# Attention and expert layer on one core: the next batch's key work moves into columns that score tiles leave empty, expert counts are read from PSUM at once, and turned logits come one slot later

## The chip, the cores and the metric

The kernel runs on 1 core of one Trainium2 chip, as one program. The metric is the device time in microseconds (us), the median of several executions. Five engines work side by side and meet at semaphores: TensorE (PE; its weight loads are shown as PEld), VectorE (DVE), ScalarE (ACT), GpSimd (POOL) and SyncE (SP), which here only starts transfers. Each engine runs its own instructions strictly in the order of the program.

## The reference

```python
B, C, Hh, Ww = (4, 128, 384, 32)                     # 4 batches of 12288 tokens, 128 wide
kv_pool = kv.reshape(B, H//4, 4, W//4, 4, C).mean(axis=(2, 4))
k = v = kv_pool.reshape(B, -1, C) @ w_sr             # 768 keys a batch, keys and values alike
s = scale * (q @ k.transpose(0, 2, 1));  s = s - s.max(-1, keepdims=True)
a = np.exp(s);  a /= a.sum(-1, keepdims=True) + 1e-09
x = (a @ v).reshape(B * S, D)
logits = x @ w_gate;  e_idx = np.argmax(logits, axis=1)     # 8 experts, one a token
gate_w = softmax(logits)[e_idx];  eom = sigmoid(x @ w_output_gate)
out[e_idx == e] = gate_w * eom[:, e] * (np.maximum(x @ w1[e], 0) @ w2[e])   # 128 -> 1024 -> 128
```

## The kernel before

**Groups, steps, slots.** The 49152 tokens are cut into 96 groups of 512, 24 to a batch. The main loop takes one group `i` a step; a step has 8 slots `s`, and `now[0]` is `8 * i + s`. Products are made of high and low fp16 halves, so that three matmuls stand for one in fp32. In one step TensorE makes the scores of group i (`qk`, one block `j` of 128 tokens in each even slot, six matmuls of 384 columns), the products with the values of group i-1 (`pv`, 18 matmuls of 512 columns in slots 5 and 6), and the expert layer of group i-2, a column block `f` a slot: `moe_h` (H, first layer), and four to five blocks later `moe_y` (Y, second layer).

**One expert ahead of the others.** For each batch the kernel picks one expert from the mean of its keys (`choice`, `chosen`), loads its weights, splits them into halves (`w_split`: fp16 tiles w0 and w1, high halves on ScalarE, low halves on GpSimd) and runs it on every token. Tokens that chose another expert are put in lists in `scr` (`routing`) and done at the end.

**PSUM.** A score tile `S` is two banks of 512 columns, and its matmuls fill columns 0 to 383 of each. Columns 384 to 511 stay free; for blocks j of 2 and 3 they take the turned output of an earlier group (`moe_turn`), for blocks 0 and 1 they can take other small products: a list `hooks` holds functions with the slot from which they may run, and `qk` takes at most one for a tile. The pool `psA` has two buffers for these tiles, taken in turn; whoever asks for a tile waits until everything that read the tile two requests earlier is done. H, U (attention output), logits and turned logits share the three banks of `psH`.

**The order on each engine** is the order in which this Python code issues, with a queue to each engine: in a slot the letters of `ORD` ("shxryfue") go through scores, moe_h, exponentials, rounding, moe_y, values and at last `e`, the functions noted for this slot with `at`. After these come the generators: the weights' split, the next keys (`kp`, one piece a slot), and the routing.

**A score block's chain** is: six matmuls into S; DVE takes the largest (`nm`, L489 and L490); ACT the exponentials into `pr` (L504), which reads S last for blocks 0 and 1; ACT rounds (`ph`, L517), POOL makes the low half (L518), SP turns it (PT). For blocks 2 and 3 DVE also scales the turned output out of S (`o`, L825). In moe_h ACT makes HH (L795) and DVE makes HL (L796) from H.

**The next batch's keys** (`kv_prep`, `fast=False`) are made in steps 1 or 2 to about 20 of each batch but the last, six blocks `k` of 128 keys. POOL adds up 16 pixels (L296 to L300); 5 slots later TensorE turns the sums into a psA tile of its own, `kvt` (L304); ACT scales them into `pT` (L307); two slots later TensorE multiplies with `wsr` into another psA tile, `kvk` (L239), and ACT stores kT (L240). At the end the largest key is spread over partitions through a third kind of tile, `vmp` (L330), and the keys are split into fp16 halves K2 and turned into V2.

**The routing** (`routing`) runs for 4 groups (a unit) at a time, 25 units in all: `logits` at slot 1 of a step copies its product to `lgp` on ACT (L563), and `logits_turn`, RG = 1 slot later, turns it on TensorE (`lT`, L581). Then the generator's pieces follow: L (L611), the one-hot choice `oh` (L637), `counts` (two small matmuls of oh16 into an S tile by a hook, L642), later a copy of the counts `cnt` on DVE (L667), and at last `st` (L684) and `nd` (L695), which read that copy and the running list ends `ebase`.

Of the kernel before, what the change touches and what calls it, by code (L numbers as in the profile page):

```python
# [20 lines left out]
F32 = mybir.dt.float32  # L21
# [4 lines left out]
AF = mybir.ActivationFunctionType  # L26
ALU = mybir.AluOpType
# [3 lines left out]
ts = bass.ts  # L31

P = 128
C = 128
E = 8
# [19 lines left out]
class Cfg:  # L55
# [11 lines left out]
    RM = 1  # L67
    LAST = (3, 1)
    SK, SO = 30, 15
    RG = 1  # L70
    RSEQ = (1, 2, 1, 1)
    HJ = (0, 1)
    LC = (2, 1)
# [27 lines left out]
def body(ctx, tc, q, kv, w_sr, w_gate, w_og, w1, w2, out, cfg=Cfg):  # L101
    nc = tc.nc
    pe, act, dve, pool, sp = nc.tensor, nc.scalar, nc.vector, nc.gpsimd, nc.sync
    NB, NCH = cfg.NB, cfg.NC
    NG = NB * NCH * CG
# [12 lines left out]
    rt = ctx.enter_context(tc.tile_pool(name="rt", bufs=1))  # L118
    psA = ctx.enter_context(tc.tile_pool(name="psA", bufs=2, space=PSUM))
# [7 lines left out]
    ident = cst.tile([P, P], F32, name="ident")  # L127
    make_identity(nc, ident)
    wsr = cst.tile([P, C], F32, name="wsr")
# [9 lines left out]
    w8 = cst.tile([P, E], F32, name="w8")  # L139
# [3 lines left out]
    ebase = cst.tile([P, E], F32, name="ebase")  # L143
# [24 lines left out]
    def largest(m, ps):  # L168

        dve.tensor_reduce(out=m, in_=ps, op=ALU.max, axis=AX.X)  # L170
        dve.scalar_tensor_tensor(m, m, 2.0 ** -100, m, op0=ALU.max, op1=ALU.max)
# [27 lines left out]
    KVN = [[0, 0] for _ in range(NB)]  # L199
# [31 lines left out]
    def kv_prep(b, fast):  # L231

        kT = kvp.tile([P, NK], F32, tag="kT", bufs=1, name=f"kT{b}")
        mx = kvp.tile([P, 8], F32, tag="vmx", name=f"vmx{b}")
        vs = kvp.tile([P, NKB], F32, tag="vs", name=f"vs{b}")
        def keys(k, ps, pT):

            kk = ts(k, P)
            pe.matmul(ps[:, 1, 0:P], wsr, pT, start=True, stop=True)  # L239
            act.activation(kT[:, kk], ps[:, 1, 0:P], AF.Copy, accum_out=vs[:, k:k + 1])  # L240
# [33 lines left out]
        for k in range(NKB):  # L274
            while KVN[b][0] < 4 * (k + 1) or not fast and now[0] < KVI[(b, k)] + cfg.KVD:
                yield
            if fast:
                if k + 1 < NKB:
                    kv_add(b, k + 1)
                x, y = kvst.pop((b, k))  # L280
                ps = psA.tile([P, 2, 512], F32, tag="A", name=f"kvt{b}_{k}")
                for h, v in enumerate((x, y)):
                    for m in range(4):
                        pe.matmul(ps[:, 0, 0:P], v[:, 0, ts(m, P)], ident, start=(h == 0 and m == 0), stop=(h == 1 and m == 3))
                pT = kvp.tile([P, P], F32, tag="pT", name=f"pT{b}_{k}")
                act.activation(pT, ps[:, 0, 0:P], AF.Copy, scale=1.0 / 16.0)
                if last:
                    keys(*last)
                last = (k, ps, pT)
                if k < NKB - 1:  # L290
                    yield
                continue
            x, y = kvst.pop((b, k))
            for v in (x[:, 1, :], y[:, 0, :], y[:, 1, :]):
                spare["n"] += 1
                pool.tensor_tensor(x[:, 0, :], x[:, 0, :], v, op=ALU.add)  # L296
                yield
            spare["n"] += 1
            pool.tensor_tensor(x[:, 1, 0:256], x[:, 0, 0:256], x[:, 0, 256:512], op=ALU.add)
            pool.tensor_tensor(y[:, 1, 0:128], x[:, 1, 0:128], x[:, 1, 128:256], op=ALU.add)  # L300
            for _ in range(5):
                yield
            ps = psA.tile([P, 2, 512], F32, tag="A", name=f"kvt{b}_{k}")
            pe.transpose(ps[:, 0, 0:P], y[:, 1, 0:128], ident)  # L304
            KVN[b][1] += 1
            pT = kvp.tile([P, P], F32, tag="pT", name=f"pT{b}_{k}")
            act.activation(pT, ps[:, 0, 0:P], AF.Copy, scale=1.0 / 16.0)  # L307
            yield
            yield
            keys(k, psA.tile([P, 2, 512], F32, tag="A", name=f"kvk{b}_{k}"), pT)  # L310
            yield
        e2 = kvp.tile([P, 7], F32, tag="ve2", name=f"ve2{b}")

        if fast:
# [9 lines left out]
        mxb = kvp.tile([P, P], F32, tag="pT", name=f"mxb{b}")  # L324
        dve.tensor_copy(mxb, mx[:, 6:7].to_broadcast([P, P]))
        if not fast:
            for _ in range(3):
                yield
        ps = psA.tile([P, 2, 512], F32, tag="A", name=f"vmp{b}")
        pe.transpose(ps[:, 0, 0:P], mxb, ident)  # L330
        if fast:
            mean()
            choice(ps[:, 1, 0:E])
            next(QP[1])
            warm(cfg.WM[1])
        largest(e2[:, 5:6], ps[:, 0, 0:P])
        powers(e2[:, 0:1], e2[:, 1:2], e2[:, 5:6])
        dve.tensor_scalar(e2[:, 2:3], e2[:, 1:2], 2.0 ** 14, None, op0=ALU.mult)
        if fast:
# [119 lines left out]
        dve.tensor_tensor(qf[:, 1, :], ps, qf[:, 0, :], op=ALU.subtract)  # L459

    hooks, now, mid = [], [0], [False]
    spare = {"n": 0}

    def qk(i, j):
# [118 lines left out]


    WF = {}
    SCT = set()

    def bc(ap2, n):
# [5 lines left out]
    def routing(c):  # L594
        g0, ng = UN[c]
# [4 lines left out]
        cho = CHO[bt]  # L600
# [5 lines left out]
        def T3(nm, n=E, bufs=1):  # L606
            return T(nm, n, F32, bufs).rearrange("p (b e) -> p b e", e=n)
# [7 lines left out]
        vs = KVT[bt][3]  # L615
# [23 lines left out]
        ps = []  # L639

        def counts(S):
            pe.matmul(S[:, 0, 384:384 + E], ones16, oh16, start=True, stop=True)  # L642
            pe.matmul(S[:, 1, 384:384 + E], tri16, oh16, start=True, stop=True)
            ps.append(S)

        ending = g0 + ng + 2 >= NG
        cnt = rt.tile([P, 2, E], F32, tag="cnt", name=f"cnt{c}")
        if ending:
            for _ in range(cfg.LC[c == NU - 1]):
                yield  # L650
            counts(psA.tile([P, 2, 512], F32, tag="A", name=f"cps{c}"))
            dve.tensor_copy(cnt, ps[0][:, :, 384:384 + E])
        else:
            hooks.append((now[0] + 1, counts))
        se = T("se")
        dve.tensor_reduce(out=se, in_=dn, op=ALU.add, axis=AX.X)
        zz = T3("dn")
# [5 lines left out]
        act.activation(z, z, AF.Exp, scale=-1.0)  # L663
        while not ps:
            yield
        if not ending:
            dve.tensor_copy(cnt, ps[0][:, :, 384:384 + E])  # L667
        yield
        dve.scalar_tensor_tensor(z, z, 1.0, sume, op0=ALU.add, op1=ALU.mult)
        dve.scalar_tensor_tensor(z, se, EPS, z, op0=ALU.add, op1=ALU.mult)  # L670
# [9 lines left out]
        x = T("x0", E)  # L680
        dve.tensor_tensor_scan(x, runs[ng], ohf, 0.0, op0=ALU.mult, op1=ALU.add)
        yield
        st = rt.tile([P, E], F32, tag="st", name=f"st{c}")
        dve.scalar_tensor_tensor(st, cnt[:, 1, :], -1.0, ebase, op0=ALU.add, op1=ALU.add)  # L684
        x1 = T3("x1")
        dve.tensor_tensor(x1, x.rearrange("p (e b) -> p b e", e=E), bb(st, nb), op=ALU.add)
        dve.tensor_tensor(x1, x1, oh, op=ALU.mult)
# [3 lines left out]
        idx = T("idx", 1, I32, 3)  # L691
        dve.scalar_tensor_tensor(idx, sel, BIG, ix, op0=ALU.mult, op1=ALU.add)

        nd = rt.tile([P, E], F32, tag="nd", name=f"nd{c}")
        dve.scalar_tensor_tensor(nd, w8, cho, cnt[:, 0, :], op0=ALU.not_equal, op1=ALU.mult)  # L695
        dve.tensor_tensor(ebase, ebase, nd, op=ALU.add)
        rw = T3("rw", RW, 3)
        pool.tensor_copy(rw[:, :, 0:1], scl.unsqueeze(2))
        for n, t0, b in ((1, tok0, CT * cc), (2, row0, 2 * CT * cc), (3, row0, 2 * CT * cc + GB)):
# [286 lines left out]
    with tc.manual_schedule(engines={pool.engine, sp.engine, pe.engine, act.engine, dve.engine}):  # L986
# [24 lines left out]
        rts, kl, kp, ws = [], None, None, None  # L1011
# [5 lines left out]
        def k0(i):  # L1017
            return cfg.KV0[min(i // GPB, 1)]

        events = {}  # L1020

        def at(n, f, *args):
            events.setdefault(8 * i + s + n, []).append((f, *args))

        def after_values(ri, rc):
            if rc is not None:
                logits(rc)

                def turn():
                    logits_turn(rc)  # L1030
                    rts.append([routing(rc), 0, rc])
                at(cfg.RG, turn)
            n = max(0, 8 * cfg.UD + cfg.UDS * ri - now[0])
            at(cfg.UT + n, u_turn, ri)
            at(cfg.UO + n, u_out, ri)
# [34 lines left out]
        for i in range(NG + OL):  # L1070
            att = i < NG
            pvi, ri, mi, oi = i - 1, i - 2, i - LAG, i - OL - 1
# [153 lines left out]
```

## Time and profile before

| what | value |
|---|---|
| time, median of 3 runs (lowest to highest) | 1962.98 us (1962.57 to 1963.02) |
| profiled execution: its own time, span from first to last instruction | 1944.66 us, 1942.9 us |
| granted TensorE clock, mean | 0.993 |
| busy: PE, PEld | 1870.8 us (96%), 951.0 us (49%) |
| busy: DVE, ACT, POOL | 1504.7 us (77%), 1321.3 us (68%), 1159.8 us (60%) |
| DMA: bytes, mean rate | 311.63 MB, 160 GB/s |

A busy share is the share of the span in which an engine was executing. TensorE's matmuls overlap, and their ends are modelled, so a gap in its row is time in which nothing ran there at all.

### The profile page before, as it was taken

How to read it: one execution, taken by the hardware profiler on the slowest of the kernel's cores; microseconds unless marked ns; L12 is line 12 of the kernel's file. 1: busy time of each engine (PE TensorE's matmuls, PEld its weight loads, DVE VectorE, ACT ScalarE, POOL GpSimd, SP SyncE). 2: the span in 40 equal slices, each digit the busy share in tenths (PEclk: the TensorE clock that was granted, in tenths of full speed). 3: DMA queues.
4: the chain of work that ended last, by engine and by line, in shares of the span. 5: the costliest groups of instructions: out<-in, count | busy, mean ns of one | idle time of the engine just before them, and what ended most of it. 6: DMA issues, size and time to landing. Idle time of an engine off the chain costs nothing. (4 is left out here: it accounts for less than half of the span.)

```text
span 1942.9 us, 31028 instructions
## 1 busy us (share of the span) xinstructions
PE 1870.8 (96%) x10225; PEld 951.0 (49%) x10225; DVE 1504.7 (77%) x3005; ACT 1321.3 (68%) x2391; POOL 1159.8 (60%) x996
## 2 busy tenths in 40 slices
PE   6999999999999999999999999999999999999997
PEld 4444455454445544545444554444445555545544
DVE  6776877888878778788787787787877877877773
ACT  3767767676776766676767776667677767767653
POOL 2537566564675676754756656656466456466462
PEclk9999999999999999999999999999999999999999
DMA  8877788788988887878788988778778778786642
GB/s 234 161 153 160 168 163 180 153 163 169 183 170 165 170 178 159 168 145 187 141 168 172 187 174 169 162 155 151 167 148 167 152 147 166 154 159 142 133 105 70
DMA packets 884017, 311.63 MB, mean 160 GB/s; under 512 B 827584, under 2 KB 833857, under 8 KB 883856
## 3 DMA queue, kind: packets, MB, share of 16 engines
q1 hardware_dynamic: 870944, 309.18, 78.7%
q0 software_dynamic: 12480, 0.40, 0.5%
q8 instruction: 81, 1.33, 0.3%
q14 instruction: 80, 0.66, 0.1%
q10 hardware_dynamic: 432, 0.07, 0.0%
HBM read 56.83 MB, written 51.25 MB: 56 GB/s over the span
## 5 line engine op out<-in xcount | busy, mean ns | idle before, releaser
L518 POOL TENSOR_TENSOR ph<-pr,ph 128x768 f16<-128x768 f32 x384 | 633.0, 1649 | 629.5 <-ACT ph L517 383.2
L796 DVE SCALAR_TENSOR_TENSOR HL<-H,HH 128x512 f16<-128x512 f32 x768 | 526.0, 686 | 142.3 <-ACT HH L795 127.9
L795 ACT ACTIVATE HH<-H 128x512 f16<-128x512 f32 x768 | 456.5, 594 | 246.6 <-PE H L792 240.3
L504 ACT ACTIVATE pr<-S,nm,qm 128x768 f32<-128x768 f32 x384 | 381.0, 992 | 240.2 <-DVE nm L490 222.7
L705 POOL DMA_INDIRECT scr<-rw,idx x384 | 383.1, 998 | 95.8 <-issue 88.1
L489 DVE TENSOR_REDUCE nm<-S 128x1 f32<-128x768 f32 x384 | 365.3, 951 | 86.8 <-PE S L487 86.3
L540 PE MATMUL U<-PT,V 128*128 128x512 f16 (+1 forms) x1746 | 406.1, 378 | 7.4 <-DVE HL L796 5.1
L517 ACT ACTIVATE ph<-pr 128x768 f16<-128x768 f32 x380 | 319.9, 842 | 2.4 <-DMA PT<-ph 1.9
L790 PE MATMUL H<-U,w 128*128 128x512 f16 x768 | 292.3, 381 | 12.3 <-DVE HL L796 7.0
L791 PE MATMUL H<-U,w 128*128 128x512 f16 x768 | 292.1, 380 | 0.0
L807 PE MATMUL Y<-HL,w 128*128 128x512 f16 x768 | 291.3, 379 | 0.7 <-DVE HL L796 0.6
L792 PE MATMUL H<-U,w 128*128 128x512 f16 x768 | 291.7, 380 | 0.0
L805 PE MATMUL Y<-HH,w 128*128 128x512 f16 x768 | 291.4, 379 | 0.3 <-ACT ys L810 0.3
L806 PE MATMUL Y<-HH,w 128*128 128x512 f16 x768 | 291.3, 379 | 0.0
L540 PEld LDWEIGHTS <-V 128*128 128x128 f16 x1746 | 171.4, 98 | 212.6 <-issue 11.5
L483 PE MATMUL S<-K,qT 128*128 128x384 f16 x768 | 189.2, 328 | 13.1 <-ACT pr L504 7.5
L487 PE MATMUL S<-K,qT 128*128 128x384 f16 x768 | 189.0, 328 | 1.3 <-DVE qT L459 1.0
L485 PE MATMUL S<-K,qT 128*128 128x384 f16 x768 | 188.9, 328 | 0.5 <-DVE K L349 0.5
L825 DVE TENSOR_TENSOR o<-S,msw 128x256 f32<-128x256 f32 x176 | 74.8, 425 | 89.0 <-ACT pr L504 87.6
L792 PEld LDWEIGHTS <-w 128*128 128x128 f16 x768 | 75.3, 98 | 91.4 <-issue 1.4
L807 PEld LDWEIGHTS <-w 128*128 128x128 f16 x768 | 75.2, 98 | 90.8 <-issue 0.3
L805 PEld LDWEIGHTS <-w 128*128 128x128 f16 x768 | 75.2, 98 | 88.3 <-issue 0.5
(209 smaller groups left out, 1865.4 us busy)
## 6 DMA issues: line engine op xcount, KB each, us to landing
kvs<-in_kv_dram SPq DMA_DIRECT2D x96, 256.0 KB
q<-in_q_dram SPq DMA_DIRECT2D x96, 256.0 KB
urows<-uT SPq DMA_DIRECT2D x96, 256.0 KB
out_dram<-o SPq DMA_DIRECT2D x96, 256.0 KB
PT<-ph SPq DMA_TRANSPOSE x384
scr<-rw,idx POOLq DMA_INDIRECT x384
wr<-in_moe_w_dram SPq DMA_DIRECT2D x8, 512.0 KB
tw<-in_moe_w_dram SPq DMA_DIRECT2D x4, 512.0 KB
```

The source lines that it names most:

```text
L489: dve.tensor_reduce(out=nm[:, 0:1], in_=S[:, :, 0:384], op=ALU.max, axis=AX.XY, negate=True)
L504: act.activation(pr.rearrange("p (a k) -> p a k", a=2), S[:, :, 0:384], AF.Exp, bias=nm[:, 1:2], scale=es, accum_out=SUMS[c][:, bl:bl + 1])
L517: act.activation(ph[:, 0, :], pr, AF.Copy)
L518: pool.tensor_tensor(ph[:, 1, :], pr, ph[:, 0, :], op=ALU.subtract)
L540: pe.matmul(PVP[i][:, cols], ops[n][0], ops[n][1][:, cols], start=(n == 0), stop=(n == len(ops) - 1))
L705: ins = pool.indirect_dma_start(out=scr, out_offset=bass.IndirectOffsetOnAxis(ap=idx[:, bl:bl + 1], axis=0), in_=rw[:, bl, :], in_offset=None,
L790: pe.matmul(H, w1h[:, ts(f, P)], UH, start=True, stop=False)
L792: pe.matmul(H, w1l[:, ts(f, P)], UH, start=False, stop=True)
L795: act.activation(HH, H, AF.Relu)
L796: dve.scalar_tensor_tensor(HL, H, 0.0, HH, op0=ALU.max, op1=ALU.subtract)
L805: pe.matmul(Y, w2h[:, ts(f, P)], HH, start=(f == 0), stop=False)
L807: pe.matmul(Y, w2h[:, ts(f, P)], HL, start=False, stop=(f == NFB - 1))
```

## The change

Four edits. (1) The sums of a key block are turned into columns 384 to 511 of a score tile, by a hook, and so is the product with `wsr`, by a second hook three slots after the first was served; `kvt` and `kvk` are gone, and ACT reads both out of the score tile right behind the exponentials of the same slot. (2) The largest key of the next batch goes the same way, and `vmp` is gone there. (3) `st` and `nd` are taken from the counts in the score tile in the slot in which it was made (`places`), and the copy `cnt` is gone; the counts' hook may run three slots after it was noted, not one. (4) `logits_turn` comes 2 slots after `logits` (1 for the last four groups); where that is an odd slot, the routing's first piece follows it at once.

```diff
-    RG = 1
+    RG = (1, 2)
...
-            for _ in range(5):
-                yield
-            ps = psA.tile([P, 2, 512], F32, tag="A", name=f"kvt{b}_{k}")
-            pe.transpose(ps[:, 0, 0:P], y[:, 1, 0:128], ident)
-            KVN[b][1] += 1
+            for _ in range(4):
+                yield
             pT = kvp.tile([P, P], F32, tag="pT", name=f"pT{b}_{k}")
-            act.activation(pT, ps[:, 0, 0:P], AF.Copy, scale=1.0 / 16.0)
-            yield
-            yield
-            keys(k, psA.tile([P, 2, 512], F32, tag="A", name=f"kvk{b}_{k}"), pT)
-            yield
+            done = []
+
+            def sums(S):
+                pe.transpose(S[:, 0, 384:512], y[:, 1, 0:128], ident)
+                at(0, scaled_sums, S)
+
+            def scaled_sums(S):
+                act.activation(pT, S[:, 0, 384:512], AF.Copy, scale=1.0 / 16.0)
+                KVN[b][1] += 1
+                done.append(0)
+
+            def product(S):
+                pe.matmul(S[:, 0, 384:512], wsr, pT, start=True, stop=True)
+                at(0, kept, S)
+
+            def kept(S):
+                act.activation(kT[:, ts(k, P)], S[:, 0, 384:512], AF.Copy, accum_out=vs[:, k:k + 1])
+                done.append(0)
+
+            hooks.append((now[0] + 1, sums))
+            while not done:
+                yield
+            hooks.append((now[0] + 3, product))
+            while len(done) < 2:
+                yield
...
+            def spread(S):
+                pe.transpose(S[:, 0, 384:512], mxb, ident)
+                done.append(S[:, 0, 384:512])
+
+            hooks.append((now[0] + 1, spread))
+            while not done:
+                yield
+            vmp = done[0]
...
+        def places(S):
+            assert NPL[0] == c
+            dve.scalar_tensor_tensor(st, S[:, 1, 384:384 + E], -1.0, ebase, op0=ALU.add, op1=ALU.add)
+            dve.scalar_tensor_tensor(nd, w8, cho, S[:, 0, 384:384 + E], op0=ALU.not_equal, op1=ALU.mult)
             ps.append(S)
...
-            hooks.append((now[0] + 1, counts))
+            hooks.append((now[0] + 3, lambda S: (counts(S), at(0, places, S))))
...
-        if not ending:
-            dve.tensor_copy(cnt, ps[0][:, :, 384:384 + E])
...
-                at(cfg.RG, turn)
+                    if now[0] % 2 and att:
+                        rts[-1][1] = 1
+                        next(rts[-1][0])
+                at(cfg.RG[ri < NG - 4], turn)
```

Three places show what the change does to the order. The first is TensorE's queue at step 19, where the last key block of the second batch (kvs1_5) is turned in front of the second score block (S19_1). Before:

```order
L806 MATMUL Y16_4524<-HH16_2_4460,w10_515 128x512
L807 LDWEIGHTS w10_515
L807 MATMUL Y16_4524<-HL16_2_4461,w10_515 128x512
L304 MATMUL kvt1_5_4554<-ident_80,kvs1_5_3867 128x128
L483 LDWEIGHTS qT19_4166
L483 MATMUL S19_1_4561<-K20_347,qT19_4166 128x384
L483 LDWEIGHTS qT19_4166
```

Changed:

```order
L845 MATMUL Y16_4506<-HH16_2_4444,w10_515 128x512
L846 LDWEIGHTS w10_515
L846 MATMUL Y16_4506<-HL16_2_4445,w10_515 128x512
L307 MATMUL S19_1_4540<-ident_80,kvs1_5_3849 128x128
L518 LDWEIGHTS qT19_4147
L518 MATMUL S19_1_4540<-K20_347,qT19_4147 128x384
L518 LDWEIGHTS qT19_4147
```

The transpose of the sums stands in the same place, but it writes into S19_1 itself, so no tile is taken between S19_0 and S19_1.

The second is VectorE's queue at step 34, where unit 7 reads its counts; nm34 and HL31 are the score maxima and the first layer's low halves. Before:

```order
L489 TENSOR_REDUCE nm34_0_8143<-S34_0_8134 128x1
L490 TENSOR_SCALAR nm34_0_8143<-nm34_0_8143,qm8_6477 128x1
L796 SCALAR_TENSOR_TENSOR HL31_0_8151<-H31_0_8146,HH31_0_8150 128x512
L415 TENSOR_REDUCE qm9_7435<-q39_7866 128x1
L421 SCALAR_TENSOR_TENSOR qm9_7435<-qm9_7435,c13_123 128x4
L422 RECIPROCAL qm9_7435<-qm9_7435 128x4
L667 COPY cnt7_8051<-S34_0_8134 128x16
L796 SCALAR_TENSOR_TENSOR HL31_1_8171<-H31_1_8166,HH31_1_8170 128x512
```

Changed (S34_0 carries the sums of a key block, so the counts go to S34_1):

```order
L835 SCALAR_TENSOR_TENSOR HL31_1_8134<-H31_1_8129,HH31_1_8133 128x512
L524 TENSOR_REDUCE nm34_1_8156<-S34_1_8147 128x1
L525 TENSOR_SCALAR nm34_1_8156<-nm34_1_8156,qm8_6449 128x1
L835 SCALAR_TENSOR_TENSOR HL31_2_8164<-H31_2_8159,HH31_2_8163 128x512
L687 SCALAR_TENSOR_TENSOR st7_8017<-S34_1_8147,ebase_98 128x8
L688 SCALAR_TENSOR_TENSOR nd7_8018<-w8_94,ch1_5493,S34_1_8147 128x8
L835 SCALAR_TENSOR_TENSOR HL31_3_8177<-H31_3_8172,HH31_3_8176 128x512
L524 TENSOR_REDUCE nm34_2_8197<-S34_2_8187 128x1
```

The copy cnt7 behind the work on query maxima (qm9) is gone, and st7 and nd7 stand right behind the HL of the slot in which their score tile was made.

The third is GpSimd's queue at steps 25 to 27, where the low halves of the second batch's weights (w11, second layer) are made; kvs2_0 is the first key block of the third batch, rw5 and scr belong to the routing. Before:

```order
L518 TENSOR_TENSOR ph25_3_6212<-pr25_3_6183,ph25_3_6212 128x768
L778 TENSOR_TENSOR w11_5791<-wr1_5326,w11_5791 128x512
L518 TENSOR_TENSOR ph26_0_6261<-pr26_0_6242,ph26_0_6261 128x768
L778 TENSOR_TENSOR w11_5791<-wr1_5326,w11_5791 128x512
L518 TENSOR_TENSOR ph26_1_6310<-pr26_1_6283,ph26_1_6310 128x768
L518 TENSOR_TENSOR ph26_2_6361<-pr26_2_6340,ph26_2_6361 128x768
L296 TENSOR_TENSOR kvs2_0_5958<-kvs2_0_5958 128x512
L698 COPY rw5_6429<-scl5_6296 128x16
L700 TENSOR_SCALAR rw5_6429<-tok0_104 128x16
L700 TENSOR_SCALAR rw5_6429<-row0_108 128x16 x2
L518 TENSOR_TENSOR ph26_3_6445<-pr26_3_6406,ph26_3_6445 128x768
```

Changed:

```order
L553 TENSOR_TENSOR ph26_3_6417<-pr26_3_6379,ph26_3_6417 128x768
L296 TENSOR_TENSOR kvs2_0_5932<-kvs2_0_5932 128x512
L817 TENSOR_TENSOR w11_6020<-wr1_5535,w11_6020 128x512
L744 DMA scr_78<-rw5_6401,idx5_6398 394240x4
L553 TENSOR_TENSOR ph27_0_6466<-pr27_0_6446,ph27_0_6466 128x768
L296 TENSOR_TENSOR kvs2_0_5932<-kvs2_0_5932 128x512
L817 TENSOR_TENSOR w11_6020<-wr1_5535,w11_6020 128x512
L553 TENSOR_TENSOR ph27_1_6508<-pr27_1_6489,ph27_1_6508 128x768
```

The two low halves of w11 have moved behind ph26_3 and ph27_0, four ph further on, each behind an addition of key pixels. On TensorE the first matmul that reads w11 (Y24, block 0) stands where it stood, behind H24_4, between the score blocks S27_1 and S27_2.

## Rows read from the trace of the kernel before

**Rows 1.** Busy time in four stretches, steps 7 to 95; stretch, length, engines (instructions), clock, DMA

```profile
165.00:479.00 314.00, 307.99 (x1689) 155.96 (x1687) 251.95 (x488) 217.83 (x398) 197.04 (x168) 1.00 0.84 169
479.00:944.00 465.00, 451.54 (x2464) 227.10 (x2462) 372.67 (x721) 325.02 (x593) 295.35 (x251) 1.00 0.83 166
944.00:1411.00 467.00, 454.01 (x2476) 228.59 (x2475) 368.33 (x718) 325.83 (x592) 295.98 (x252) 1.00 0.84 166
1411.00:1852.00 441.00, 439.59 (x2418) 221.86 (x2416) 344.78 (x676) 317.00 (x561) 259.60 (x217) 1.00 0.78 152
```

**Rows 2.** TensorE's waits, whole span: who waits for whom, us, times, longest

```profile
PE S L483 <- ACT pr L504: 7.5, 6, 1.7
PE H L790 <- DVE HL L796: 7.0, 12, 1.3
PE S L822 <- ACT pr L504: 6.6, 5, 2.5
...
PE S L642 <- DVE oh L637: 3.6, 1, 3.6
PE S L483 <- DVE cnt L667: 2.8, 2, 1.7
...
PE lT L581 <- ACT lgp L563: 1.6, 3, 0.5
```

**Rows 3.** The same view from 30 to 60 us alone

```profile
PE S L483 <- ACT pr L504: 3.5, 3, 1.5
```

**Rows 4.** Timeline of TensorE at step 19: start, length, instruction, idle before

```profile
386.47 0.27 PE L304 MATMUL kvt<-ident,kvs 128*128 128x128 f32 x1
388.44 0.32 PE L483 MATMUL S<-K,qT 128*128 128x384 f16 x1 [1.70 <-ACT pr L504]
```

**Rows 5.** Timeline of ScalarE at the same place

```profile
387.31 0.99 ACT L504 ACTIVATE pr<-S,nm,qm 128x768 f32<-128x768 f32 x1 [1.57 <-DVE nm L490]
```

**Rows 6.** Busy time in two short stretches (columns as in rows 1)

```profile
126.60:133.20 6.60, 5.86 (x18) 2.37 (x19) 4.67 (x9) 2.07 (x4) 1.64 (x1) 0.50 0.81 152
775.10:778.40 3.30, 3.30 (x11) 1.67 (x12) 0.82 (x1) 1.81 (x3) 2.98 (x3) 0.50 1.01 213
```

**Rows 7.** Timeline of TensorE where the second batch's Y24 begins

```profile
541.23 0.38 PE L805 MATMUL Y<-HH,w 128*128 128x512 f16 x1
541.44 0.38 PE L806 MATMUL Y<-HH,w 128*128 128x512 f16 x1
```

**Rows 8.** Timeline of GpSimd in the same stretch

```profile
539.54 1.64 POOL L518 TENSOR_TENSOR ph<-pr,ph 128x768 f16<-128x768 f32 x1 [3.49 <-issue]
541.14 2.60 POOL L296 TENSOR_TENSOR kvs<-kvs 128x512 f32<-128x512 f32 x2
```

**Rows 9.** Groups by line: count | busy, mean ns of one | idle before, and who ended it

```profile
L825 DVE TENSOR_TENSOR o<-S,msw 128x256 f32<-128x256 f32 x176 | 74.8, 425 | 89.0 <-ACT pr L504 87.6 <-DMA PT<-ph 1.4
...
L684 DVE SCALAR_TENSOR_TENSOR st<-cnt,ebase 128x8 f32<-128x8 f32 x25 | 18.8, 754 | 0.0
L778 POOL TENSOR_TENSOR w<-wr,w 128x512 f16<-128x512 f32 x16 | 18.6, 1164 | 1.1 <-ACT w L774 1.0
...
L695 DVE SCALAR_TENSOR_TENSOR nd<-w,ch,cnt 128x8 f32<-128x8 f32 x25 | 5.5, 219 | 0.0
...
L667 DVE COPY cnt<-S 128x16 f32<-128x16 f32 x23 | 3.4, 147 | 1.2 <-ACT pr L504 1.2
```

**Rows 10.** Busy time in the 6 us behind those two waits of cnt

```profile
450.40:456.40 6.00, 6.00 (x32) 2.99 (x30) 4.94 (x11) 4.65 (x9) 2.77 (x2) 1.00 0.90 213
1826.10:1832.10 6.00, 6.00 (x33) 3.09 (x32) 5.25 (x14) 5.06 (x11) 2.76 (x2) 1.00 0.79 170
```

**Rows 11.** Timeline of VectorE behind the counts of unit 0

```profile
127.51 1.59 DVE L658 TENSOR_TENSOR dn<-L,oh 128x128 f32<-128x128 f32 x1
```

**Rows 12.** Timeline of GpSimd: the last addition of the first key block

```profile
100.59 0.45 POOL L300 TENSOR_TENSOR kvs<-kvs 128x128 f32<-128x128 f32 x1
```

**Rows 13.** Timeline of TensorE: the first matmuls of the score block S4_3

```profile
105.33 0.49 PE L483 MATMUL S<-K,qT 128*128 128x384 f16 x2
```

More of the change, by code (lines that the diff above doesn't have):

```diff
@@ L328, in kv_prep @@
                 yield
-        ps = psA.tile([P, 2, 512], F32, tag="A", name=f"vmp{b}")
-        pe.transpose(ps[:, 0, 0:P], mxb, ident)
+        if fast:
+            ps = psA.tile([P, 2, 512], F32, tag="A", name=f"vmp{b}")
+            pe.transpose(ps[:, 0, 0:P], mxb, ident)
+            vmp = ps[:, 0, 0:P]
+        else:
+            done = []
+            def spread(S):
[5 more added lines that the diff above has]
+            vmp = done[0]
         if fast:
@@ L335, in kv_prep @@
             warm(cfg.WM[1])
-        largest(e2[:, 5:6], ps[:, 0, 0:P])
+        largest(e2[:, 5:6], vmp)
         powers(e2[:, 0:1], e2[:, 1:2], e2[:, 5:6])
@@ L461, in body, with at @@
     hooks, now, mid = [], [0], [False]
+    events = {}
+    def at(n, f, *args):
+        events.setdefault(now[0] + n, []).append((f, *args))
     spare = {"n": 0}
@@ L585, in body @@
     WF = {}
+    NPL = [0]
     SCT = set()
@@ L643, in counts @@
             pe.matmul(S[:, 1, 384:384 + E], tri16, oh16, start=True, stop=True)
+        ending = g0 + ng + 2 >= NG
+        st = rt.tile([P, E], F32, tag="st", name=f"st{c}")
+        nd = rt.tile([P, E], F32, tag="nd", name=f"nd{c}")
+        def places(S):
+            assert NPL[0] == c
+            dve.scalar_tensor_tensor(st, S[:, 1, 384:384 + E], -1.0, ebase, op0=ALU.add, op1=ALU.add)
+            dve.scalar_tensor_tensor(nd, w8, cho, S[:, 0, 384:384 + E], op0=ALU.not_equal, op1=ALU.mult)
             ps.append(S)
-        ending = g0 + ng + 2 >= NG
-        cnt = rt.tile([P, 2, E], F32, tag="cnt", name=f"cnt{c}")
         if ending:
@@ L650, in routing @@
                 yield
-            counts(psA.tile([P, 2, 512], F32, tag="A", name=f"cps{c}"))
-            dve.tensor_copy(cnt, ps[0][:, :, 384:384 + E])
+            S = psA.tile([P, 2, 512], F32, tag="A", name=f"cps{c}")
+            counts(S)
+            places(S)
         else:
-            hooks.append((now[0] + 1, counts))
+            hooks.append((now[0] + 3, lambda S: (counts(S), at(0, places, S))))
         se = T("se")
@@ L665, in routing @@
             yield
-        if not ending:
-            dve.tensor_copy(cnt, ps[0][:, :, 384:384 + E])
         yield
@@ L682, in routing @@
         yield
-        st = rt.tile([P, E], F32, tag="st", name=f"st{c}")
-        dve.scalar_tensor_tensor(st, cnt[:, 1, :], -1.0, ebase, op0=ALU.add, op1=ALU.add)
         x1 = T3("x1")
@@ L692, in routing @@
         dve.scalar_tensor_tensor(idx, sel, BIG, ix, op0=ALU.mult, op1=ALU.add)
-        nd = rt.tile([P, E], F32, tag="nd", name=f"nd{c}")
-        dve.scalar_tensor_tensor(nd, w8, cho, cnt[:, 0, :], op0=ALU.not_equal, op1=ALU.mult)
         dve.tensor_tensor(ebase, ebase, nd, op=ALU.add)
+        NPL[0] = c + 1
         rw = T3("rw", RW, 3)
@@ L1018, in k0 @@
             return cfg.KV0[min(i // GPB, 1)]
-        events = {}
-        def at(n, f, *args):
-            events.setdefault(8 * i + s + n, []).append((f, *args))
         def after_values(ri, rc):
```

## The prediction

> **What bounds the kernel now.** I read the busy times by stretch first. Four stretches cover steps 7 to 23, 24 to 47, 48 to 71 and 72 to 95, a batch each [rows 1]. TensorE is busy nearly all the time in every one, while VectorE, the next, has a fifth of its time free; so time is won or lost only where TensorE stands still. The reader should compare the last stretch with the others: it has no next keys to prepare, and there TensorE idles 441.00 - 439.59 = 1.4 us, against 6.0, 13.5 and 13.0 us in the three that prepare keys. What goes with preparing the next batch costs some 30 us of TensorE's idle time.
>
> The list of TensorE's waits says what ends them [rows 2]. Three kinds are waits of a score tile for its buffer: the first matmul of S behind an exponential (L483 behind L504), the turned output in front of it (L822 behind L504), and S behind the copy of the counts (L667). A score tile has two buffers, and in the plain run of blocks the tile two requests earlier is four slots old, long done. At step 19 one sees what a third customer does [rows 4, 5]: kvt takes the buffer between S19_0 and S19_1, so S19_1 gets the buffer of S19_0, whose exponentials have only just begun; TensorE idles 1.70 us until they end.
>
> **Change, part by part: what it removes.**
> *Buffer waits.* Of the six waits of L483 behind exponentials three (3.5 us) fall into the first 60 us, which the edit does not touch [rows 3]. 7.5 - 3.5 = 4.0 us, the five of L822 (6.6) and the two behind cnt (2.8) remain: 13.4 us in 10 waits [rows 2]. In the timeline each of the ten stands close behind a kvt, kvk or vmp matmul, as at step 19. A wait also loses the overlap of a matmul with the next, 0.38 us long but begun 0.21 us after the one before [rows 7]: 10 x 0.17 = 1.7. Together 15.1 us. With kvt, kvk and vmp gone, 13 requests a batch, only score tiles take the two buffers.
>
> *The clock behind the long ones.* Two of those waits reach 2.5 us (the longest, rows 2). Behind the one that ends at 774.96 the granted clock is 0.50 for 3.3 us with TensorE busy for all of it: 1.2 in place of 2.4 GHz [rows 6]. Half of 3.3 us is lost, and the same once more at 1239 us: 3.3 us.
>
> *Counts of unit 0.* In the first steps a hook may use any block, and the counts went to S5_3 while VectorE was still making oh: 3.6 us [rows 2], then 6.6 us at half clock with 5.86 us of work [rows 6], half of it lost, and 0.17: 6.7 us. With a start three slots on they go to S6_0. But VectorE's burst stays: behind it comes an L658 of 1.59 us [rows 11], and TensorE would wait for an HL soon after. I count half: 3.3 us.
>
> *Turned logits one slot later.* The three waits for lgp go: 1.6 + 3 x 0.17 = 2.1 us [rows 2].
>
> Sum of what goes: 15.1 + 3.3 + 3.3 + 2.1 = 23.8 us.
>
> **What it adds and moves.**
> *Hooks in the score tiles.* TensorE's instructions are the same in number. The transpose of the sums now stands in front of a score block, so a late POOL would hold the scores too; the least room is at S4_3, where POOL's additions end at 100.59 + 0.45 = 101.04 and the block begins at 105.33 [rows 12, 13]: 4.3 us. No wait. The readings on ACT stand behind the exponentials of their own tile, and that buffer is asked for again four slots later. Cost: nothing; if that cover went, the buffer waits above would come back.
>
> *Everything for the next batch about a step later*, since a block waits for a block 0 or 1 twice. K2, V2 and the expert's choice still come two steps before their batch. The weights of the second batch don't have that room: the low halves of w11 now stand behind ph26_3 and one key addition on POOL. The ph ends at 541.18, half of two additions is 1.30 us [rows 8], a low half 1.16 [rows 9]: 543.6. Y24 needs it with its second matmul, at 541.44 [rows 7]: 2.2 us, and ScalarE's high half, now ahead of ph26_3, pushes that to some 2.4. It may halve the clock again (the waits of 2.5 us did, that of 1.70 did not), up to 1.65 us; I take 3.2 us in all. In the later batches TensorE comes to the new weights more than a step after they are made.
>
> *Counts read at once.* st and nd now stand right behind the HL of their slot, and read the banks that the exponentials read. o (L825) is in that place in before, and idles 87.6 us behind L504 in 176 instances, 0.5 us each; the two copies of cnt that fell so early idled 0.6 each [rows 9]. So st will wait 0.5 to 0.6 us, 23 times. The Trainium skill (PSUM — Partial Sum Buffer, PSUM bank collisions raise a hardware error) says why: two engines may not touch one bank and quadrant at once, reads included, so a dependency is put between them. By that rule alone 23 x 0.6 = 14 us would be added to VectorE's queue, and the trace agrees with the wait. What it costs TensorE is another question: in the 6 us behind each of the two early copies it was busy for 6.00 of 6.00 us [rows 10]. st itself lasted 754 ns in the mean and the copy 147 [rows 9]; from PSUM I expect it near the copy, and nd is as before. [...] Bounds for the 23 places: nothing, up to 0.61 + 0.75 + 0.22 - 0.15 = 1.4 us each if st keeps its mean and all of it reaches TensorE. I take nothing, by rows 10, the nearest case.
>
> *Given back.* TensorE gets ahead of VectorE by what it no longer loses, and its waits for HL (7.0 us in 12, rows 2) may grow. The last stretch, which runs without buffer waits, idles only 1.4 us, so I take 2.6 us, a tenth.
>
> **Sum.** 23.8 - 3.2 - 2.6 = 18 us. The profiled execution took 1944.66 us (span 1942.9), and would take 1926.7. The median of the three runs is 18.3 us above it; 18 us off that is 1945.
>
> **Rivals.**
> *The waits move on.* For it: many of TensorE's other waits in batches with key work end with an HL or U of VectorE, whose bursts (maxima, weights, routing) stay. If half of 15.1 + 3.3 comes back as waits for HL, the counts of unit 0 give nothing and the weights cost 4: 23.8 - 9.2 - 3.3 - 4.0 = 7 us, 1956. Against: the last stretch.
>
> *Slower: VectorE held at 23 places.* If st keeps its length and the delay reaches TensorE, 23 x 1.4 = 32 us are added: 1945 + 32 = 1977. It decides once more than 18 / 23 = 0.8 us of each reaches TensorE. For it: the wait is certain, and where qm stands ahead of the next HL that slot is full already. Against: rows 10.
>
> *No change.* The buffer waits go, and TensorE meets ScalarE's exponentials a block later instead, since it runs ahead of the chain of maxima, exponentials and rounding: 1963. Against: no such wait stands in the last stretch.
>
> *All of it.* Nothing is given back, unit 0 gives 6.7, and ScalarE brings the weights in time: 23.8 + 3.4 + 2 = 29 us, 1934.
>
> **How the numbers follow.** My forecast (a gain of 12 to 25 us, 1938 to 1951) gets 0.58, all of it 0.08, the waits that move on (4 to 12 us) 0.21, no change 0.07, slower 0.06. 0.2% is 4 us, about what can be told from no change here. Faster: 0.58 + 0.08 + 0.21 = 0.87. The range goes from 1936, inside the best case, to 1957, which takes in most of the case in which waits move on; both ends of the weights' price lie in it.
>
> **What would show it.** Right: no wait of S for an exponential or counts after 60 us; idle time in the three stretches down to 1 to 6 us each; a granted clock of 1.00 at 775 and 1239 us; a wait of 2 to 3 us at Y24 for POOL; st near 0.2 us with an idle time of 0.5 us ahead of it, ended by L504. Wrong: TensorE's waits for HL grown by more than 5 us; waits for HL right behind the 23 places of st; the counts of unit 0 replaced by an equal wait for VectorE.

## The result: 0.75% slower, and the profile after

The changed kernel takes 1977.67 us (median of 4 runs, 1976.51 to 1978.66), the kernel before, run beside it, 1962.83 (1962.57 to 1963.02). The ratio is 1.0075, with a 95% interval from 1.0058 to 1.0093: slower by some 15 us, where 18 us of gain were forecast. In a second comparison it was 1.0093 (1.0077 to 1.0108).

One thing is needed to read the spans. In some sets of runs the ending, from the end of the last score block, lasts some 102 to 105 us, in others 90, whichever kernel runs: the kernel before has medians of 1940.8, 1942.6, 1960.3 and 1962.8 us in four sets, and its profile, at 1944.66, is one with the short ending, that of the changed kernel (span 1975.7) one with the long. So kernels are compared below by their ratios to the kernel before on the same chip, and profiles up to the last score block, which ends at 1852.8 us before and at 1870.6 after: 17.8 us later. These two profiles are of different sets, so a few of the 17.8 us may belong to the set: ahead of the ending, too, one kernel differs between sets by some us (the block ends at 1870.6 us in one profile of the changed kernel and at 1875.3 in the other).

The four stretches of [rows 1], cut at nearly the same steps in the changed kernel (length, then busy time of TensorE, its weight loads, VectorE, ScalarE, GpSimd, then the granted clock):

```profile
167.00:482.00 315.00, 305.41 (x1660) 153.99 (x1659) 245.08 (x477) 216.22 (x396) 197.77 (x168) 0.99 0.85 166
482.00:949.00 467.00, 450.21 (x2465) 227.18 (x2464) 371.77 (x709) 321.13 (x586) 291.35 (x247) 1.00 0.83 166
949.00:1419.00 470.00, 456.01 (x2478) 229.29 (x2477) 373.19 (x713) 322.83 (x590) 295.54 (x252) 0.99 0.84 165
1419.00:1870.00 451.00, 441.68 (x2421) 221.98 (x2420) 351.35 (x677) 318.04 (x565) 261.85 (x219) 1.00 0.76 148
```

Read the last one first. It has no key work, so the first two edits do nothing in it; before, TensorE idled 1.4 us there. Now it idles 451.00 - 441.68 = 9.3 us and the stretch is 10 us longer. More than half of the loss thus has nothing to do with the keys. What TensorE waits for, from 60 us to the last score block (as in [rows 2]):

```profile
PE H L829 <- DVE HL L835: 33.2, 31, 2.4
PE H L829 <- DVE U L580: 10.3, 18, 1.0
PE U L575 <- DVE HL L835: 5.8, 7, 1.8
PE Y L845 <- POOL w L817: 2.5, 1, 2.5
PE Y L844 <- ACT ys L849: 1.5, 5, 0.4
```

The same view of the kernel before, for the waits behind VectorE:

```profile
PE H L790 <- DVE HL L796: 6.7, 11, 1.3
...
PE U L540 <- DVE HL L796: 5.1, 6, 1.7
PE H L790 <- DVE U L545: 4.7, 11, 1.0
```

Every wait of S for an exponential or for the copy of the counts is gone (13.4 us), and so is that of the counts for oh (3.6 us) and, but for 0.2 us in the whole span, those for lgp. But the waits for HL and for the low half of U, both of VectorE, have grown from 6.7 and 4.7 us in the same part of the span to 33.2 and 10.3. So VectorE is late. Its groups by line say with what (count, busy time, mean ns of one):

```profile
L652 DVE SCALAR_TENSOR_TENSOR sume<-SUM,ve 128x16 f32<-128x16 f32 (+2 forms) x25 | 24.4, 976 | 0.0
L726 DVE TENSOR_TENSOR x<-x,st 128x128 f32<-128x128 f32 (+2 forms) x25 | 21.2, 848 | 0.0
...
L727 DVE TENSOR_TENSOR x<-x,oh 128x128 f32<-128x128 f32 (+2 forms) x25 | 15.1, 605 | 0.9
...
L687 DVE SCALAR_TENSOR_TENSOR st<-S,ebase 128x8 f32<-128x8 f32 x23 | 3.8, 167 | 13.7 <-ACT pr L539 13.7
```

The same view of the kernel before, for the lines that [rows 9] doesn't hold:

```profile
L686 DVE TENSOR_TENSOR x<-x,st 128x128 f32<-128x128 f32 (+2 forms) x25 | 12.8, 512 | 0.9
...
L687 DVE TENSOR_TENSOR x<-x,oh 128x128 f32<-128x128 f32 (+2 forms) x25 | 9.4, 375 | 0.9
...
L616 DVE SCALAR_TENSOR_TENSOR sume<-SUM,ve 128x16 f32<-128x16 f32 (+2 forms) x25 | 8.4, 337 | 0.0
```

Two things stand in these rows. The sum of exponentials (sume) is 16 us longer, with the same shape. And st, 15 us shorter as forecast, has handed its time on: st and the two x1 lines together took 18.8 + 12.8 + 9.4 = 41.0 us and take 4.1 + 21.2 + 15.1 = 40.4 (with the two short st of the end); x1, the next instruction in line whose tensors all lie in SBUF, now starts beside GpSimd's ph in 14 of 25 units. The timeline of VectorE in the last batch, a first routing piece of the changed kernel, and GpSimd beside it:

```profile
1600.80 0.41 DVE L647 COPY L<-lT 128x256 f32<-128x256 f32 x1
1601.25 0.42 DVE L648 TENSOR_TENSOR L<-L,lT 128x256 f32<-128x256 f32 x1
1601.59 1.11 DVE L652 SCALAR_TENSOR_TENSOR sume<-SUM,ve 128x16 f32<-128x16 f32 x1
1602.73 0.25 DVE L653 RECIPROCAL rinv<-sume 128x16 f32<-128x16 f32 x1
```

```profile
1601.03 1.65 POOL L553 TENSOR_TENSOR ph<-pr,ph 128x768 f16<-128x768 f32 x1 [2.33 <-ACT ph L552]
```

The sum handles 16 columns and starts in the middle of ph, which ends at 1601.03 + 1.65 = 1602.68; it ends at 1602.70. In 19 of 25 units it starts so, during ph, and lasts 1.05 to 1.24 us; in one more it starts at the end of an indirect DMA of GpSimd with ph right behind, and lasts 2.23. In the kernel before the same piece runs in slot 2, the sum at 1586.10 with nothing of GpSimd beside it:

```profile
1586.10 0.23 DVE L616 SCALAR_TENSOR_TENSOR sume<-SUM,ve 128x16 f32<-128x16 f32 x1
1586.36 0.25 DVE L617 RECIPROCAL rinv<-sume 128x16 f32<-128x16 f32 x1
```

### The profile page after: what moved, and what is told of

The parts are those of the page before. It is cut to its first block, busy times and chain, and to the rows that moved or that the text cites. A ratio compares the mean times of both kernels' runs of the same rounds, so it can differ in the third digit from the quotient of the medians.

```text
span 1975.7 us, 30969 instructions
## 1 busy us (share of the span) xinstructions
PE 1875.2 (95%) x10225; PEld 952.3 (48%) x10225; DVE 1513.7 (77%) x2980; ACT 1315.5 (67%) x2391; POOL 1160.8 (59%) x996
## 5 line engine op out<-in xcount | busy, mean ns | idle before, releaser
L575 PEld LDWEIGHTS <-V 128*128 128x128 f16 x1746 | 171.3, 98 | 214.0 <-issue 12.8
```

The lines of the kernel that those rows point to most:

```text
L575: pe.matmul(PVP[i][:, cols], ops[n][0], ops[n][1][:, cols], start=(n == 0), stop=(n == len(ops) - 1))
```

## The experiments

The theory from these rows: the fourth edit puts the sum beside GpSimd's ph of slot 3, where it is held until ph ends, and TensorE pays for it through HL and U. Rivals: the counts' part (st, nd, the later chain behind them), or the burst a slot later as such.

**The last edit undone.**

```diff
-    RG = (1, 2)
+    RG = 1
...
-                    if now[0] % 2 and att:
-                        rts[-1][1] = 1
-                        next(rts[-1][0])
-                at(cfg.RG[ri < NG - 4], turn)
+                at(cfg.RG, turn)
```

> The changed kernel without its last edit: the logits are turned in slot 2 of a step again and the first routing piece stands in that slot; the rest of the change stays. Theory A: the last edit is the loss, because the first piece now runs beside GpSimd's ph of an odd slot, and its sum of exponentials (L652), with two inputs from SBUF, lasts 1.11 us in 19 of 25 units where it took 0.23; 16 us on VectorE's queue, in front of HL and U. Then this kernel takes 1945 to 1960 us, less than before (1962.8), and the sum is back at 0.23 us. Rival B: the counts read at once and the later chain behind them are the loss (x1 at L726 went from 370 to 1143 ns in the median). Then this kernel stays at 1972 to 1978 us. Half and half: 1965.

Measured: 1930.84 us, where the kernel before takes 1940.83; ratio 0.9948 (0.9933 to 0.9964). The times in the expectation were set against 1962.8; by ratio the gain of 0.5% lies in theory A's range. The sum takes 7.2 us in all, and TensorE's waits for HL 11.5 (these totals, here and in the runs below, are over the whole span). The first three edits gain 10 us.

**The last edit alone**, added to the kernel before (the same lines the other way).

> The kernel before with the last edit alone (logits turned and first routing piece in slot 3). Theory A: slower than before by 12 to 18 us, 1975 to 1981 us, with the sum of exponentials near 1.1 us in most units. Rival B: 1961 to 1965 us.

Measured: 1970.84 against 1940.83, ratio 1.0156 (1.0138 to 1.0173): 30 us, more than expected. The sum takes 28.2 us. The last edit is the loss, with or without the rest.

**The sum moved to slot 4**, the last edit kept.

```diff
-        dve.scalar_tensor_tensor(sume, SUM, vs[:, 0:1], vs[:, 1:2].to_broadcast([P, nb]), op0=ALU.mult, op1=ALU.add)
-        dve.reciprocal(rinv, sume)
         yield
...
         dve.tensor_tensor(d, L[:, :, 0:E], bc(mx, E), op=ALU.subtract)
+        dve.scalar_tensor_tensor(sume, SUM, vs[:, 0:1], vs[:, 1:2].to_broadcast([P, nb]), op0=ALU.mult, op1=ALU.add)
+        dve.reciprocal(rinv, sume)
```

> The changed kernel with its last edit kept, but the sum of exponentials and its reciprocal moved from the first routing piece (slot 3) to the second (slot 4, behind mx and d), where no ph of GpSimd runs. Theory A in its narrow form (the held sum alone): about as the kernel without the last edit, 1943 to 1960 us, the sum at 0.23 us. Theory A in its wide form (the whole burst of routing being a slot later): 1970 to 1978 us though the sum is short. Rival B: also 1970 to 1978 us, with the kernel without the last edit there too.

Measured: 1939.63, ratio 0.9991 (0.9982 to 0.9999), the sum at 0.23 us. By ratio this lies at the upper edge of what was expected of the held sum alone (0.990 to 0.999), and below the other form (1.004 to 1.008). Against the changed kernel's 1.0093 (run again below) two short instructions in another slot give back 1.0%, 20 us, against its 1.0075 above 0.8%, 16 us. It is not quite the kernel without the last edit (0.9948): 0.43%, some 8 us, stay with the rest of the last edit, about the wide form's share. What in it costs these was not taken apart; the waits for HL are 19.5 us here and 11.5 there, while VectorE is busy for 1498.7 us here and 1499.0 there, so VectorE has no more work, only the same work at another place.

**The keys' part alone** (first two edits).

> The kernel before with the first part of the change alone: sums, products and maxima of the next keys in the empty columns of score tiles; counts and logits as before. By the prediction's terms (10 buffer waits, 15.1 us, and 3.3 us of half clock behind two of them, less up to 3.2 us for the low half of w1 in the second batch) a gain of 12 to 18 us: 1945 to 1951 us. Rival, the waits move on to HL and U: 1956 to 1963 us.

Measured: 1933.98, ratio 0.9965 (0.9952 to 0.9978), a gain of 7 us: between the two, at the rival's edge. The waits from 60 us to the last score block, with VectorE's sum as in the kernel before:

```profile
PE H L825 <- DVE HL L831: 10.1, 14, 1.8
PE H L825 <- DVE U L580: 6.7, 12, 1.0
PE U L575 <- DVE HL L831: 5.5, 7, 1.7
PE S L677 <- DVE oh L672: 3.8, 1, 3.8
PE lT L616 <- ACT lgp L598: 3.2, 6, 0.8
PE Y L841 <- POOL w L813: 2.5, 1, 2.5
```

The 13.4 us of buffer waits are gone, and so are the half-clock periods at 775 and 1239 us; one of 3.4 us at 441 us is new. Of the waits 3.4 us came back as waits for HL, 2.0 for U, 1.6 for lgp, and 2.5 at Y24.

**The changed kernel once more**, on a chip of its own set.

> The changed kernel as it is, beside the other runs, so that its loss is known under the same conditions. The last edit cost the kernel before 30 us when added alone, and the change without it gains 10 us. If the two add up, 1930.8 + 30 = 1961 us, 1.010 of before. If what it costs depends on the rest (the same held sum, but buffer waits that take some of it in), 1945 to 1958 us.

Measured: 1978.50 against 1960.32, ratio 1.0093 (1.0077 to 1.0108). By ratios the last edit takes 1.0093 / 0.9948 = 1.0146 on top of the other three, and 1.0156 on the kernel before: the two add up nearly.

**The sum with one tensor input.** Every instruction in its place; a form with one tensor and two operands per partition.

```diff
-        dve.scalar_tensor_tensor(sume, SUM, vs[:, 0:1], vs[:, 1:2].to_broadcast([P, nb]), op0=ALU.mult, op1=ALU.add)
+        dve.tensor_scalar(sume, SUM, vs[:, 0:1], vs[:, 1:2], op0=ALU.mult, op1=ALU.add)
```

> The changed kernel with its last edit kept and every instruction in its place; only the sum of exponentials is written as a tensor_scalar with two operands per partition, so that one tensor comes from SBUF in place of two. Theory (the sum is held by GpSimd's ph because it reads two tensors from SBUF): it lasts 0.1 to 0.25 us beside the same ph, and the time is that of the kernel with the sum in slot 4, 1935 to 1944 us. Rival (what is held is whatever stands there, or the slot itself is the cost): the sum stays near 1.1 us or the time within 3 us of the changed kernel run beside it.

Measured: 1976.75, ratio 1.0087 (1.0073 to 1.0101), no different from the changed kernel. The row says why:

```profile
L652 DVE TENSOR_SCALAR sume<-SUM,ve 128x16 f32<-128x16 f32 (+2 forms) x25 | 24.7, 988 | 0.0
```

It is held just as long, so the run doesn't speak against the hold: it refutes my narrower form of it, two tensors from SBUF. The Trainium skill (SBUF — State Buffer, Who interferes with whom) has tensor_scalar among the operations that can take both of VectorE's ports with a single input, when its operands meet that mode's conditions, and then contend with GpSimd. The trace agrees as to the hold (1.11 us beside ph, 0.29 with nothing beside it); that the instruction ran in such a mode no run shows.

**The sum alone in slot 3.** The last edit undone, the sum and its reciprocal one slot later by themselves.

```diff
+        def total():
+            dve.scalar_tensor_tensor(sume, SUM, vs[:, 0:1], vs[:, 1:2].to_broadcast([P, nb]), op0=ALU.mult, op1=ALU.add)
+            dve.reciprocal(rinv, sume)
+
+        if g0 + ng + 2 >= NG:
+            total()
+        else:
+            at(1, total)
```

> The changed kernel without its last edit (1930.8 us), with the sum of exponentials and its reciprocal alone moved from slot 2 to slot 3. Theory (the held sum): it lasts 1.1 us in most units again, and the time is 10 to 21 us above 1930.8, that is 1941 to 1952 us. Rival (the turned logits and their burst a slot later are the cost, the held sum only shows it): within 3 us of 1930.8.

Measured: 1948.35 against 1960.32, ratio 0.9942 (0.9929 to 0.9956): as without the move, and the sum takes 6.8 us in all. That is the rival's number, but the theory was not put to the test, since the sum was not held: the expectation was wrong about where it would lie. Without the two instructions on L ahead of it the sum begins 0.17 to 0.30 us before ph in 18 units (not some 13, as the next expectation has it) and is over about when ph begins; in one it began 0.23 us behind and lasted 1.44. So slot 3 as such costs the sum nothing; which side of ph's start it falls on may. The next pair crosses that line.

**The sum just behind ph's start, and just ahead of it.** As the last run, with two reductions mx in slot 3 (one is from slot 4, the second only takes time).

```diff
+        def total():
+            dve.tensor_reduce(out=mx, in_=L[:, :, 0:E], op=ALU.max, axis=AX.X)
+            dve.tensor_reduce(out=mx, in_=L[:, :, 0:E], op=ALU.max, axis=AX.X)
+            dve.scalar_tensor_tensor(sume, SUM, vs[:, 0:1], vs[:, 1:2].to_broadcast([P, nb]), op0=ALU.mult, op1=ALU.add)
+            dve.reciprocal(rinv, sume)
```

> The changed kernel without its last edit, where slot 3 now holds two reductions mx (one would do; the second only takes 0.28 us), then the sum of exponentials and its reciprocal. In the run with the sum alone in slot 3 it began 0.2 us before GpSimd's ph in about 13 of 23 units and lasted 0.23; behind 0.57 us of reductions it begins some 0.35 us after ph, and by the theory (held until ph ends) lasts some 1.3 us in 12 to 20 units, 13 to 22 us on VectorE's queue. Theory: 0.7 to 1.2% above its twin with the same instructions in the other order. Rival (the hold shows in VectorE's times, but TensorE doesn't pay for it; the last edit's loss is the burst a slot later): within 0.2% of the twin.

The twin has the last two lines first.

> The twin: the same instructions in slot 3, the sum and its reciprocal first, then the two reductions. Theory: the sum lasts 0.23 us as in the run with the sum alone in slot 3, and the time is 0.993 to 0.998 of before (0.994 without the extra reductions; two of 0.28 us, one of them new, in 23 units). Rival: as the other order.

Measured against 1942.58: 1948.44, ratio 1.0028 (1.0019 to 1.0037), with the reductions first; 1929.73, ratio 0.9929 (0.9917 to 0.9942), with the sum first. The same instructions in the same slot, 1.0% apart, 18.7 us. VectorE and GpSimd with the reductions first:

```profile
1589.30 0.28 DVE L655 TENSOR_REDUCE mx<-L 128x16 f32<-128x128 f32 x1
...
1589.52 1.64 POOL L553 TENSOR_TENSOR ph<-pr,ph 128x768 f16<-128x768 f32 x1 [2.43 <-ACT ph L552]
...
1589.61 0.29 DVE L656 TENSOR_REDUCE mx<-L 128x16 f32<-128x128 f32 x1
...
1589.81 1.38 DVE L657 SCALAR_TENSOR_TENSOR sume<-SUM,ve 128x16 f32<-128x16 f32 x1
```

and with the sum first:

```profile
1573.80 0.23 DVE L655 SCALAR_TENSOR_TENSOR sume<-SUM,ve 128x16 f32<-128x16 f32 x1
...
1574.02 1.65 POOL L553 TENSOR_TENSOR ph<-pr,ph 128x768 f16<-128x768 f32 x1 [2.43 <-ACT ph L552]
...
1574.06 0.25 DVE L656 RECIPROCAL rinv<-sume 128x16 f32<-128x16 f32 x1
...
1574.23 0.23 DVE L657 TENSOR_REDUCE mx<-L 128x16 f32<-128x128 f32 x1
```

TensorE's waits for HL, over the whole span, with the reductions first and with the sum first:

```profile
PE H L837 <- DVE HL L843: 23.4, 26, 2.1
```

```profile
PE H L837 <- DVE HL L843: 12.1, 15, 1.6
```

A hundredth of the kernel hangs on half a microsecond. The sum takes 29.8 us in the first and 6.9 in the second, and of these 22.9 us TensorE pays 18.7, as forecast: its waits for HL are 23.4 and 12.1, for U 9.2 and 6.9, and the rest, as far as the profiles tell, is half clock (five periods of 3.4 us ahead of the ending against three) and the overlap that each wait loses. The rival, that the hold shows in VectorE's times only, falls.

**The counts' part alone** (third edit).

> The kernel before with the counts' part of the change alone: counts three slots after oh, st and nd read them from PSUM at once. Theory: st is short but the hold by GpSimd passes to x1, which now stands first there, so VectorE gains nothing; TensorE gains at most the wait for unit 0's oh (3.6 us and 3.3 us of half clock). 1934 to 1940 us. Rival (st and nd hold up the next HL at 23 places, 0.6 us and more each): 1945 to 1955 us. The prediction's own terms: a gain of 3.3 us, 1937.5.

Measured: 1958.22 against 1960.32, ratio 0.9991 (0.9982 to 1.0000). A gain of 2 us, hardly to be told from none, and within the theory's range (the times in the expectation were set against 1940.8); VectorE's st waits 14.1 us for the exponentials in it, and TensorE doesn't pay. On top of the keys' part (0.9965 to 0.9948) it gives 3 us.

**A held instruction of the kernel before freed.** The last edit undone, and the product of the gate's logits with oh, 1.48 us beside ph in both kernels, put behind oh. The product before:

```profile
L702 DVE TENSOR_TENSOR dn<-L,oh 128x128 f32<-128x128 f32 (+2 forms) x25 | 35.8, 1434 | 0.9
...
L705 DVE TENSOR_TENSOR z<-z,rinv 128x16 f32<-128x16 f32 (+2 forms) x25 | 6.3, 250 | 0.9
```

```diff
+        zz = T3("zz")
+        dve.tensor_tensor(zz, L[:, :, E:2 * E], oh, op=ALU.mult)
         oh16 = rt.tile([P, E], F16, tag="oh16", name=f"oh16{c}")
...
-        zz = T3("dn")
-        dve.tensor_tensor(zz, L[:, :, E:2 * E], oh, op=ALU.mult)
```

> The changed kernel without its last edit, with one more instruction taken from beside GpSimd's ph: the product of the output gate's logits and oh (1.48 us in the median beside ph, in before and after alike) stands right behind oh, in a buffer of its own, half a microsecond or more ahead of ph. Theory (an instruction of VectorE on SBUF alone is held until ph ends, and TensorE pays for it through HL and U): it lasts 0.38 to 0.5 us, about 1.0 us less in 23 units, and the time falls by 8 to 23 us below 0.994 of before: 0.982 to 0.990. Rival (the hold isn't on TensorE's path there, or passes to the next instruction): 0.992 to 0.996.

Measured: 1919.52 against 1942.58, ratio 0.9876 (0.9860 to 0.9892), 0.7% or 14 us below the kernel without the last edit, within the theory's range. The same two lines here:

```profile
L705 DVE TENSOR_TENSOR z<-z,rinv 128x16 f32<-128x16 f32 (+2 forms) x25 | 20.7, 828 | 0.9
...
L672 DVE TENSOR_TENSOR zz<-L,oh 128x128 f32<-128x128 f32 (+2 forms) x25 | 9.2, 369 | 0.9
```

Of the 26.6 us taken off the product 14.4 passed on to the product of z with rinv, which now starts during ph (at 1570.52 us, 0.87 behind ph's start, it lasts 0.81 in place of 0.17). VectorE's busy time fell by 15.8 us (1499.0 to 1483.2), so nearly all that VectorE gained reached the end; TensorE's waits for HL fell from 11.5 to 6.0 us, those of H for U from 7.0 to 3.6. That the hold passes to the next instruction, the rival's reason, is thus true of half of it.

**And the second batch's weights two slots earlier.**

```diff
-        T = now[0] + (cfg.WTN if b else cfg.WT0)
+        T = now[0] + ((8 if b == 1 else cfg.WTN) if b else cfg.WT0)
```

> The kernel with the early product, and the weights of the second batch split two slots earlier, so that TensorE's wait of 2.5 us for the low half of w1 at Y24, which the prediction priced at 3.2 us, should go. By that price 0.0016 below the kernel with the early product alone; if the earlier split only makes other work late, the same or above.

Measured: 1916.80, ratio 0.9863 (0.9846 to 0.9879). The wait at Y24 is gone from TensorE's list; the difference of 0.0013 (2.7 us by the medians) is near the expected 0.0016, but the intervals overlap. This version beats both kernels, by 1.4% the one before.

## Why the prediction was wrong

**The step that failed** is "Turned logits one slot later. The three waits for lgp go: 1.6 + 3 x 0.17 = 2.1 us." It priced only what the edit removes. The 2.1 us did go (lgp 0.2 us after), but the move took the first routing piece from slot 2 to slot 3, where GpSimd runs ph, and there its sum is held: 16 us on VectorE. The edit costs 25 to 30 us in all (1.0156 alone, 1.0128 or 1.0146 on top of the rest by the two comparisons of the changed kernel). 16 to 20 of them are the held sum, shown by moving it off slot 3, and by the twins on either side of ph's start, 18.7 us apart; some 8 more go with the rest of the piece, and their cause stays open. The prediction had a hold of VectorE among its rivals for st alone. By the Trainium skill (SBUF — State Buffer, Who interferes with whom) an instruction of VectorE with two inputs from SBUF contends with one of GpSimd that reads SBUF; asked of each instruction of the moved piece, with the row of ph beside slot 3, that names the sum, and the trace agrees (1.11 us in place of 0.23).

**Buffer waits.** Right in mechanism: all ten are gone, and the clock is 1.00 at 775 and 1239 us (in the changed kernel it halves at 443, 992 and 1074 us instead, for 3.4 to 6.8 us, around the new waits for HL). Wrong in size: 15.1 + 3.3 less 3.2 for the weights and 2.6 given back make 12.6 us; alone the two edits gained 7. The term that was too small is the last: 3.4 + 2.0 + 1.6 = 7.0 us came back as waits for HL, U and lgp, not 2.6. The rival in which waits move on was nearer. In the whole change TensorE's idle time in the three stretches, forecast to fall to 1 to 6 us each, rose from 6.0, 13.5 and 13.0 us to 9.6, 16.8 and 14.0. The last stretch, from which the tenth was taken, has no maxima and no low halves of a next batch's keys on VectorE, so it was no measure for the others; that this is the reason is argued, not shown.

**The weights at Y24.** Right as to the wait: forecast 2.4 us, measured 2.49. The half clock behind it came in some runs (3.4 us long in the changed kernel's second profile) and not in others. Taking the wait away gave 2.7 of the 3.2 us by the medians, whose ratios have overlapping intervals.

**Counts.** The step on their reading was right for TensorE: st waits 0.6 us at 23 places, nothing comes of it. The slower rival, 23 x 1.4 us, gave 1977 us, the very time measured, by luck: it was not what happened, the counts' part alone is no slower. Not forecast was that st's hold passes on to x1, which then stands first behind the scan: on these lines VectorE gained 0.6 us, not 15. Unit 0's wait for oh (3.6 us) is gone; behind its burst TensorE now waits for an HL instead, as the prediction feared, 1.10 us in the counts' part alone and 2.40 in the changed kernel, in whose second profile the clock also halves there for 3.4 us. The 3.3 us counted for it are near the 2 to 3 us of this part.

**Wrong, if** ... "TensorE's waits for HL grown by more than 5 us": that sign was named, and it came, by 26.5 us; its cause, the moved piece, was not.

## What to carry to other kernels

When a piece of work is moved by a slot, list what every engine runs in the new slot, and ask of each instruction moved whether it shares a path with one of those; an edit that only waits one slot longer is a move like any other. A duration several times that of the same shape elsewhere, ending with another engine's instruction, is a hold, and moving the instruction half a microsecond may be worth more than removing waits. Where a held instruction is made cheap, look at the next one in line before the saving is booked.

## What the runs showed of the hardware

Some instructions of VectorE whose operands all lie in SBUF, when they start during GpSimd's ph (1.64 us), end with it: the sum 1.11 us in place of 0.23 with two tensors, 1.11 in place of 0.29 with one tensor and two operands per partition, 1.38 where it started earlier in ph, the product 1.48 in place of 0.37. GpSimd's other additions and subtractions held it too: in the kernel before, in slot 2, it lasted 1.08 us beside an addition of key pixels and 1.34 to the end of a low half of the weights. Started 0.08 to 0.30 us ahead of ph, with GpSimd idle, the sum was not held. Where it started in the last 0.14 to 0.51 us of an indirect DMA on GpSimd's queue with ph right behind, it lasted until ph's end (1.97 and 2.00 us in the run with the reductions first, 2.23 in the changed kernel) or, with a low half of the weights right behind ph, until the end of that (2.98); with nothing right behind the DMA it took 0.23. The reciprocal (0.25 us) and the reductions (0.23 to 0.29) ran beside ph at their usual length, and so did HL, with one operand in PSUM (0.69). That a hold lasts until the other engine's whole instruction ends is also what the Trainium skill says (SBUF — State Buffer, Who interferes with whom): whoever issues first gets the pair of ports that the two engines share for the whole instruction.

The ending of 102 to 105 us in place of 90, in some sets of runs, comes with one wait of TensorE of 9.6 to 11.1 us, put down in four of five profiles to ScalarE's ys, and with a wait of GpSimd of 12 to 13 us in place of 3 for the read of its lists. What ScalarE waits for there, the trace doesn't show; it stays open.
